# Attention probabilities transposed without TensorE, and a fixed instruction order from the fourth chunk

## The chip, the cores and the metric

The kernel runs on one core of one Trainium2 chip. The metric is the device time of one execution in microseconds. The kernel before took 1209.49 us (median of 3 runs, 1207.8 to 1210.51); it is called "before" below.

## What is computed

Two stages follow each other. The first is attention of 8 batches with 8 heads, head size 64: 512 local positions attend to 32 global keys and to a band of 32 positions on either side; 32 global positions attend to all 544 keys. The second is a gated feed-forward network on all 8 × 544 = 4352 tokens, with model width 512 and inner width 1536.

```python
s_g = scale * np.matmul(q_g, k_all.transpose(0, 1, 3, 2));  out_g = np.matmul(sm(s_g), v_all)
s_ll = np.where(np.abs(pos[:, None] - pos[None, :]) <= 32, scale * q_l @ k_l^T, -1e9)
out_l = np.matmul(sm(concat([q_l @ k_g^T * scale, s_ll])), concat([v_g, v_l]))
x = concat([out_g, out_l]).transpose(0, 2, 1, 3).reshape(B * S, 512)
y = (1 / (1 + np.exp(-(x @ w_gate))) * (x @ w_val)) @ w_out
```

All of it is float32. The kernel writes a float32 operand as a rounded high part plus the rest ("hi" and "lo", type fp32r) and adds three of the four products.

## The kernel before

**Chunks.** The tokens are worked on in chunks of 512 (one batch of local tokens; batch 0 is cut into two chunks of 256, numbers 0 and 1; batches 1 to 7 are chunks 2 to 8), and the 256 global tokens come last. While the feed-forward network of one chunk runs on TensorE, the attention of the next chunk is threaded between its matmuls. The network of a chunk is a loop over 12 slices f of the inner width: 12 matmuls into bank_g and 12 into bank_v (line 385), ScalarE's Tanh, Exp and Abs and two VectorE operations make th, ScalarE and GpSimd split it into hh, and one slice later 12 matmuls (line 414) add it into the four banks bank_o. From chunk 2 on a matmul has 512 columns.

**A local unit.** A head has two local units of two 128-row query blocks each and one global unit. Heads of chunks 0 and 1 and heads 0 to 3 of chunk 2 are "native" (plain float32); the other 52 heads, 104 local units, are split into hi and lo. A local unit goes through four stages of `local_unit`: the scores (line 229, and in a head's second unit two small products of line 223), VectorE's mask and row minimum (241), ScalarE's Exp (244); the reciprocal of the row sum and the scaling by it (252, 253, 208); four TensorE transposes of 128 × 128 (264, 265) into the PSUM tile bank_y, and the split of the result into pt by ScalarE (274) and VectorE (275); four matmuls with the values (294, 295), ScalarE's copy of the lower half (297), VectorE's and GpSimd's additions (298, 299), which give x32. Two heads later `x_split` writes xt, the input of the next chunk's network. The global unit (line 330 and following) interleaves its scores with the previous head's global products (308).

**What sets the order.** Attention steps are events with a due time. The unit of time is four 512-column matmuls of the network: `ffn_stream` yields after every four, and every event that has come due by then is issued. A head's base time is 12 units after the one before it; its local units are 4 units apart, and the four stages of a unit stand 0, 3, 6 and 9 units behind its start (`STAGES`). All the instructions of a stage are issued at once. A scheduler then sets each engine's final order by its own estimates.

**Queues and buffers.** Every DMA is issued by SyncE (SP), in order. PSUM tiles bank_g, bank_v, bank_x and bank_y share four banks (tag "att"); pt has two buffers, s_buf three, ob (the output rows) four.

Of the kernel before, what the change touches and what calls it, by code (L numbers as in the profile page):

```python
# [37 lines left out]
BASE, PER = 3, 4  # L38
STAGES = (0, 3, 6, 9)
LOAD_QK, LOAD_V, SPLIT_QK, SPLIT_V = 16, 9, 10, 4  # L40
# [15 lines left out]
def kernel(ctx, tc, qk, v, w_gate, w_val, w_out, out_l, out_g):  # L56
# [28 lines left out]
    ident_r, masks_r = (const.tile([P, w], F32R, name=nm) for w, nm in ((P, "ident_r"), (256, "masks_r")))  # L85
    nc.scalar.copy(ident_r, ident)
    nc.scalar.copy(masks_r, masks[:, 0:256])
# [101 lines left out]

    def split_v(T):  # L190
        if T["native"]:
            return
        t = T["v_raw"]
        vhl = spl.tile([P, 8, 2 * D], F32R, name="vhl")
        nc.scalar.copy(vhl[:, :, 0:D], t)  # L195
        nc.gpsimd.tensor_tensor(vhl[:, :, D:2 * D], t, vhl[:, :, 0:D].bitcast(F32), op=ALU.subtract)  # L196
        T["v"] = vhl

    def warm(bank, n):

        for _ in range(n):
            nc.tensor.matmul(bank[:, 0:256], ident_r, masks_r, start=True, stop=True)
# [8 lines left out]
    def local_unit(T, blocks, x32s, h, col0):  # L211
        ks, k0s, q0 = T["qk"], T["k0"], T["q0"]
        nat = T["native"]
        last = len(ks) - 1
        s_ps = ps.tile([P, 2, 256], F32, name="bank_x", tag="att", bufs=4)
        if T["first"]:
            warm(s_ps.rearrange("p a c -> p (a c)"), 16 if h == 0 else 2)
        with_gg = T["with_g"] and blocks[-1] == 3
        if with_gg:

# [4 lines left out]
        for i, j in enumerate(blocks):  # L225
            qj = ks[0][:, qcol(j) - q0:qcol(j) - q0 + P]
            for t, (kt, k0) in enumerate(zip(ks, k0s)):
                js = slice(k0 + KOFF[j], k0 + KOFF[j] + KWIN[j])
                nc.tensor.matmul(s_ps[:, i, 0:KWIN[j]], qj, kt[:, js], start=t == 0, stop=t == last)  # L229
        if T["first"] and cnt["s"] % 2:  # L230
            s_sb = ffn.tile([P, 2, WIN], F32, name="s_first", tag="ob", bufs=4)
# [4 lines left out]
        nm = small.tile([P, 2], F32, name="nm")  # L236
        sm = small.tile([P, 2], F32, name="sm")
        r = small.tile([P, 2], F32, name="r")
        for i, j in enumerate(blocks):
            w, m = KWIN[j], 0 if j else WIN  # L240
            anchor[0] = nc.vector.tensor_tensor_reduce(  # L241
                out=s_sb[:, i, 0:w], in0=s_ps[:, i, 0:w], in1=masks[:, m:m + w], scale=-0.125, scalar=3.0e38,
                op0=ALU.add, op1=ALU.min, accum_out=nm[:, i:i + 1])
            nc.scalar.activation(s_sb[:, i, 0:w], s_sb[:, i, 0:w], AF.Exp, bias=nm[:, i:i + 1], scale=-1.0,  # L244
                                 accum_out=sm[:, i:i + 1])
        if with_gg:
            mg = T["mg"] = small.tile([SG, 4], F32, name="mg")
            nc.vector.tensor_tensor_reduce(
                out=pg[:, SL:GW], in0=gg, in1=zero.broadcast_to([SG, SG]), scale=-0.125, scalar=3.0e38,
                op0=ALU.add, op1=ALU.min, accum_out=mg[:, 0:1])  # L250
# [15 lines left out]
        if nat:  # L266
            if T["first"] and h % 2:
                pt = ffn.tile([P, 4, P], F32, name="pt_first", tag="th", bufs=2)
            else:
                pt = att.tile([P, 4, P], F32, name="pt_nat", tag="pt", bufs=2)  # L270
            nc.scalar.copy(pt, pt_ps)
        else:
            pt = att.tile([P, 2, 4, P], F32R, name="pt", bufs=2)
            nc.scalar.copy(pt[:, 0], pt_ps)  # L274
            nc.vector.tensor_tensor(pt[:, 1], pt_ps, pt[:, 0].bitcast(F32), op=ALU.subtract)  # L275
# [5 lines left out]
        dst = x32s[h // 2][prow:prow + 64, col0:col0 + 2 * P].rearrange("p (i c) -> p i c", c=P)
        if nat:
            if T["first"]:
                o_ps = ps.tile([64, 2, P], F32, name="bank_x", tag=f"bank_o{2 + h % 2}")
            else:
                o_ps = ps.tile([64, 2, P], F32, name="bank_x", tag="att", bufs=4)
            for i, j in enumerate(blocks):
                nc.tensor.matmul(o_ps[:, i], vt[:, VM[j], :], pt[:, 2 * i], start=True, stop=False)  # L288
                nc.tensor.matmul(o_ps[:, i], vt[0:sides[i], VS[j], :], pt[0:sides[i], 2 * i + 1], start=False, stop=True)
            nc.scalar.copy(dst, o_ps)  # L290
# [299 lines left out]
```

## Time and profile before

| what | value |
|---|---|
| median of the runs | 1209.49 us |
| the profiled execution, its own time and its span | 1206.77 us, 1204.7 us |
| busy: PE, DVE, ACT, POOL | 97%, 60%, 65%, 49% of the span |
| mean granted TensorE clock | 0.987 |
| DMA | 152.80 MB, mean 127 GB/s |
| end of the network of chunk 2, of chunk 3 | 402.3 us, 532.9 us |

The span runs from the first instruction to the last; the profiled execution's own time is 2.1 us more than it. PE's busy share includes the time in which a matmul's result is still on its way, so the distance between starts tells what a matmul takes from PE, and the durations do not. "PEld" is the loading of weights, which overlaps matmuls.

### The profile page before, as it was taken

To read this page: it belongs to the slowest core of one execution; us is meant where nothing else is said; L and a number is where in the kernel's file an instruction comes from. 1 tells how busy PE (TensorE), PEld (TensorE's weight loads), DVE (VectorE), ACT (ScalarE), POOL (GpSimd) and SP (SyncE) were. 2 spreads that over 40 slices of the span, in tenths; PEclk is the share of its full clock that TensorE was granted. 3 is DMA by queue.
4 is the path that set the end of the run, shared out by engine and by line. 5 is a ranking of instruction groups with operands and counts; after the bars stand their busy time and mean duration, and the time that the engine had idled before them with its cause. 6 is when DMAs were issued, how large, how long until landed. Compare 5 with 4: busy or idle time off the path is not lost.

```text
span 1204.7 us, 19673 instructions
## 1 busy us (share of the span) xinstructions
PE 1172.4 (97%) x6606; PEld 971.4 (81%) x6606; DVE 727.5 (60%) x2275; ACT 780.2 (65%) x1836; POOL 585.4 (49%) x631
## 2 busy tenths in 40 slices
PE   8887999999999999999999999999999999999998
PEld 7565778888888888888888888888888888888897
DVE  5866874756776567756765677757775677511121
ACT  6766786767677677767766767767776776532232
POOL 2442553645656366545656465636654565311111
PEclk9978899999999999999999999999999999999999
DMA  7674763433334433333334433443434332131143
GB/s 259 237 270 166 253 210 105 118 120 112 98 103 130 125 105 123 97 127 105 115 97 123 125 95 110 127 128 100 128 97 127 106 114 75 53 105 55 68 145 119
DMA packets 50277, 152.80 MB, mean 127 GB/s; under 512 B 6144, under 2 KB 7168, under 8 KB 50176
## 3 DMA queue, kind: packets, MB, share of 16 engines
q1 hardware_dynamic: 50176, 151.54, 40.2%
q8 instruction: 52, 0.85, 0.3%
q14 instruction: 49, 0.40, 0.1%
HBM read 136.31 MB, written 15.20 MB: 126 GB/s over the span
## 4 chain that ended last, share of the span: by engine, by line
PE 75%; ACT 8%; DVE 7%; issue 6%; POOL 2%; DMA 1%; SPq 0%; POOLq 0%; ACTq 0%; DVEq 0%
PE bank_g L385 20%; PE bank_o L414 19%; PE bank_v L385 18%; PE bank_x L229 5%; PE bank_x L330 3%; PE bank_x L294 2%; PE bank_y L264 2%; PE bank_y L265 2%; PE bank_x L295 2%; ACT s_buf L244 1%; PE bank_x L308 1%; DVE s_buf L208 1%; ACT pg_buf L343 1%; POOL hh L401 1%; PE bank_x L288 1%
## 5 line engine op out<-in xcount | busy, mean ns | idle before, releaser
L385 PE MATMUL bank_g<-xt,wg 128*128 128x512 f32 (+1 forms) x1440 | 337.2, 369 | 1.0 <-ACT xt L367 0.9
L385 PE MATMUL bank_v<-xt,wv 128*128 128x512 f32 (+1 forms) x1440 | 329.1, 364 | 0.0
L414 PE MATMUL bank_o<-wo,hh 128*128 128x512 f32 x1224 | 325.0, 399 | 0.3 <-ACT hh L400 0.2
L385 PEld LDWEIGHTS bank_g<-xt,wg 128*128 128x128 f32 x1440 | 239.6, 191 | 41.6 <-issue 3.0
L385 PEld LDWEIGHTS bank_v<-xt,wv 128*128 128x128 f32 x1440 | 236.3, 188 | 38.0 <-issue 1.1
L414 PEld LDWEIGHTS bank_o<-wo,hh 128*128 128x128 f32 x1224 | 219.2, 189 | 41.7 <-issue 1.1
L401 POOL TENSOR_TENSOR hh<-th,hh 128x512 fp32r<-128x512 f32 (+1 forms) x120 | 136.7, 1139 | 237.8 <-ACT hh L400 226.8
L397 DVE SCALAR_TENSOR_TENSOR bank_v<-ex,bank_v 128x512 f32<-128x512 f32 (+1 forms) x120 | 73.1, 610 | 152.1 <-PE bank_v L385 148.7
L184 POOL TENSOR_TENSOR kl<-qk_raw,qk_hi 128x736 fp32r<-128x736 f32 x52 | 92.2, 1773 | 132.9 <-ACT qk_hi L183 131.8
L244 ACT ACTIVATE s_buf<-s_buf,nm 128x192 f32<-128x192 f32 (+1 forms) x248 | 114.1, 461 | 50.2 <-DVE nm L241 47.8
L400 ACT CAST hh<-th 128x512 fp32r<-128x512 f32 (+1 forms) x120 | 66.6, 555 | 115.4 <-DVE th L398 114.7
L393 ACT ACTIVATE th<-bank_g 128x512 f32<-128x512 f32 (+1 forms) x120 | 63.4, 528 | 83.5 <-PE bank_g L385 82.6
L241 DVE CUSTOM_DVE_ANT_0 s_buf<-bank_x,masks 128x192 f32<-128x192 f32 (+1 forms) x248 | 82.3, 367 | 41.9 <-PE bank_x L229 40.4
L299 POOL TENSOR_TENSOR x<-t 64x256 f32<-64x256 f32 x104 | 77.0, 740 | 62.0 <-DVE t L298 59.4
L196 POOL TENSOR_TENSOR vhl<-v_raw,vhl 128x512 fp32r<-128x512 f32 x52 | 67.0, 1288 | 47.8 <-ACT vhl L195 45.8
L208 DVE TENSOR_SCALAR s_buf<-s_buf,r 128x224 f32<-128x224 f32 (+1 forms) x230 | 86.1, 396 | 3.8
L183 ACT CAST qk_hi<-qk_raw 128x1280 fp32r<-128x1280 f32 x52 | 65.8, 1266 | 29.1 <-PE bank_x L308 17.8
L275 DVE TENSOR_TENSOR pt<-bank_y,pt 128x512 fp32r<-128x512 f32 x104 | 71.5, 687 | 20.6 <-ACT pt L274 20.0
L298 DVE TENSOR_TENSOR t<-bank_x,t 64x512 f32<-64x512 f32 x104 | 70.7, 680 | 21.0 <-ACT t L297 17.3
L186 POOL TENSOR_TENSOR qk_hi<-qk_raw,qk_hi 64x256 fp32r<-64x256 f32 x104 | 78.8, 772 | 4.7
L252 DVE TENSOR_SCALAR r<-sm 128x2 f32<-128x2 f32 x128 | 33.5, 262 | 78.2 <-ACT s_buf L244 78.2
L398 DVE SCALAR_TENSOR_TENSOR th<-th,bank_v 128x512 f32<-128x512 f32 (+1 forms) x120 | 72.4, 603 | 6.1 <-DVE bank_v L397 0.5
(117 smaller groups left out, 2003.1 us busy)
## 6 DMA issues: line engine op xcount, KB each, us to landing
wo<-wo_dram SPq DMA_DIRECT2D x116, 512.0 KB, 3.3
qk_raw<-in_qk_dram SPq DMA_DIRECT2D x104, 320.0 KB, 4.6
v_raw<-in_v_dram SPq DMA_DIRECT2D x52, 256.0 KB, 2.6
out_dram<-ob SPq DMA_DIRECT2D x34, 256.0 KB, 3.0
xt<-in_w_gate_dram SPq DMA_DIRECT2D x12, 512.0 KB, 4.5
xt<-in_w_val_dram SPq DMA_DIRECT2D x12, 512.0 KB, 4.1
xt<-in_w_out_dram SPq DMA_DIRECT2D x12, 512.0 KB, 4.2
v_nat<-in_v_dram SPq DMA_DIRECT2D x8, 512.0 KB, 3.9
```

The costliest lines, as they stand in the source:

```text
L184: nc.gpsimd.tensor_tensor(kl, t[:, K0:Q1], hi[:, K0:Q1].bitcast(F32), op=ALU.subtract)
L186: nc.gpsimd.tensor_tensor(hi[64:128, r], t[64:128, r], hi[64:128, r].bitcast(F32), op=ALU.subtract)
L208: nc.vector.tensor_scalar(out, in_, by, None, op0=ALU.mult)
L241: anchor[0] = nc.vector.tensor_tensor_reduce(out=s_sb[:, i, 0:w], in0=s_ps[:, i, 0:w], in1=masks[:, m:m + w], scale=-0.125, scalar=3.0e38, ...
L244: nc.scalar.activation(s_sb[:, i, 0:w], s_sb[:, i, 0:w], AF.Exp, bias=nm[:, i:i + 1], scale=-1.0, accum_out=sm[:, i:i + 1])
L275: nc.vector.tensor_tensor(pt[:, 1], pt_ps, pt[:, 0].bitcast(F32), op=ALU.subtract)
L299: nc.gpsimd.tensor_tensor(dst, t0[:, :, 0], t0[:, :, 1], op=ALU.add)
L385: nc.tensor.matmul(acc, w[a][:, t, fs], xt[:, c, t, x0:x0 + ntok], start=n == 0, stop=n == 11)
L397: nc.vector.scalar_tensor_tensor(acc, ex, 1.0, acc, op0=ALU.min, op1=ALU.mult)
L398: nc.vector.scalar_tensor_tensor(th, th, 1.0, acc, op0=ALU.add, op1=ALU.mult)
L401: nc.gpsimd.tensor_tensor(hh[:, 1, 0:ntok], th, hh[:, 0, 0:ntok].bitcast(F32), op=ALU.subtract)
L414: nc.tensor.matmul(o_ps[t], ph[:, a, t * P:(t + 1) * P], pwo[:, c], start=f2 == 0 and i == 0, stop=f2 == NF - 1 and i == 2)
```

## The change

**The transposes.** In the split units `local_split` takes the place of `local_unit`. The four TensorE transposes and bank_y are gone. VectorE transposes both blocks' probabilities inside each 32 × 32 square (one instruction, 128 × 448, into the new tile tb, two buffers); four DMAs write tb into a DRAM buffer pd (three buffers) in rows of 64 numbers, 256 bytes each; two DMAs read pd back as 128 rows of 1 KB each, already in the order that the products need, into the half pt[:, 1]. ScalarE makes the hi half from it, and the subtraction that leaves the lo half is done in place, by GpSimd in a head's first unit and by VectorE in its second. The products read pt in runs of 32 numbers.

**The order.** From due time 108 on (the network of chunk 2, the attention of chunk 3) every engine's order is the order in which the program issues: the scheduler no longer moves anything. Each unit is cut into smaller steps with delays of their own (`LOCAL`, `GLOBAL`, `LAST`, `SPLIT`, in the same units of time), and a head starts 5 units earlier against the network (`BASE` 3 becomes -2).

**Smaller edits.** ob has three buffers in place of four; the warming matmuls at the start have 128 columns in place of 256 and are twice as many; the tile masks_r is gone.

```diff
-BASE, PER = 3, 4
+BASE, PER = -2, 4
+MANUAL = 108
+LOCAL = dict(reduce=0.5, exp=0.4, norm=1.7, write=1.3, read=4, hi=4, lo=0.6, pv=2, copy=0.5, add=0.6, x=0.7)
-        for i in range(2):
-            nc.tensor.transpose(pt_ps[:, 2 * i], s_sb[:, i, 0:P], ident)
-            nc.tensor.transpose(pt_ps[:, 2 * i + 1], s_sb[:, i, WIN - P:WIN], ident)
...
-            pt = att.tile([P, 2, 4, P], F32R, name="pt", bufs=2)
-            nc.scalar.copy(pt[:, 0], pt_ps)
-            nc.vector.tensor_tensor(pt[:, 1], pt_ps, pt[:, 0].bitcast(F32), op=ALU.subtract)
+        tb = att.tile([P, 7, 2, 32], F32, name="tb", bufs=2)
+        nc.vector.transpose(tb.rearrange("p b k i -> p k b i"), s_sb.rearrange("p k (b i) -> p k b i", i=32))
+        yield w["write"]
+        pd = dram.tile([7, 32, 4, 64], F32, name="pd", bufs=3)
+        for a in range(4):
+            rows = slice(32 * a, 32 * a + 32)
+            nc.sync.dma_start(pd[:, :, a].rearrange("b j r -> j b r"), tb[rows].rearrange("p b k i -> p b (k i)"))
+        yield w["read"]
+        pt = att.tile([P, 2, 2, 4, 2, 32], F32R, name="pt", bufs=2)
+        for m in range(2):
+            src = pd[3 * m:3 * m + 4].rearrange("b j a r -> (b j) (a r)")
+            nc.sync.dma_start(pt[:, 1, m].rearrange("p a k i -> p (a k i)").bitcast(F32), src)
+        yield w["hi"]
+        flat = pt.rearrange("p c m a k i -> p c (m a k i)")
+        nc.scalar.copy(flat[:, 0], flat[:, 1].bitcast(F32))
+        yield w["lo"]
+        (nc.vector if blocks[0] else nc.gpsimd).tensor_tensor(
+            flat[:, 1], flat[:, 1].bitcast(F32), flat[:, 0].bitcast(F32), op=ALU.subtract)
+        yield w["pv"]
...
+            nc.tensor.matmul(out, vt[:, VM[j], :], pt[:, :, 0, :, i, :], start=True, stop=False)
+            nc.tensor.matmul(out, vt[0:side, VS[j], :], pt[0:side, :, 1, :, i, :], start=False, stop=True)
...
-                            ob = ffn.tile([P, DM], F32, name="ob", bufs=4)
+                            ob = ffn.tile([P, DM], F32, name="ob", bufs=3)
...
+    def step(gen):
+        d = next(gen, None)
+        if d is not None:
+            put(now[0] + d, 2, lambda: step(gen))
+    def start(gen, at_once=True):
+        if now[0] >= MANUAL or not at_once:
+            step(gen)
+        else:
+            for _ in gen:
+                pass
...
     for dt in ffn_stream(items):
-        now += dt
-        while queue and queue[0][0] <= now:
-            queue.pop(0)[2]()
+        catch_up(now[0] + dt)
+        if now[0] >= MANUAL and MANUAL not in cnt:
+            cnt[MANUAL] = region.enter_context(tc.manual_schedule())
+    region.close()
```

**How the order moves.** First TensorE, in the middle of a chunk, around one slice's matmuls into bank_v (wv) and bank_o. Before, a unit's four transposes (lines 264, 265, read from s_buf) stand between them:

```order
L385 MATMUL bank_v<-xt,wv_118 128x512 x3
L264 MATMUL bank_y<-ident,s_buf_107 128x128 [waits DVE_49]
L265 MATMUL bank_y<-ident,s_buf_107 128x128
L264 MATMUL bank_y<-ident,s_buf_107 128x128 [waits DVE_49]
L265 MATMUL bank_y<-ident,s_buf_107 128x128
L385 MATMUL bank_v<-xt,wv_119 128x512 x4
```

After, network matmuls, a unit's scores (231) and another unit's products (353, 354) are all that is there, and the products carry a wait on DMA queues beside those on engines:

```order
L231 MATMUL bank_x<-qk_hi 128x192 [waits DVE_49]
L231 MATMUL bank_x<-kl,qk_hi 128x192
L231 MATMUL bank_x<-qk_hi 128x224
L231 MATMUL bank_x<-kl,qk_hi 128x224
L487 MATMUL bank_g<-xt,wg_114 128x512 x4
L487 MATMUL bank_v<-xt,wv_116 128x512 [waits DVE_49]
L487 MATMUL bank_v<-xt,wv_116 128x512 x3
L487 MATMUL bank_v<-xt,wv_117 128x512 x4
L353 MATMUL bank_x<-pt,vhl 128x256 [waits DMAHW6_49,DVE_49,Pool_49]
L354 MATMUL bank_x<-pt,vhl 128x256 [waits DMAHW7_49]
L353 MATMUL bank_x<-pt,vhl 128x256
L354 MATMUL bank_x<-pt,vhl 128x256
```

From the scores of a unit to its own products PE now has 60 network matmuls of 512 columns, two other units' scores (one of them with the two small products), two other units' products and one global unit with its products; before, the due times put 9 units (36 network matmuls) between them.

Second, SyncE's queue, for about one head in the middle of a chunk. Before:

```order
L405 DMA wo<-wo_dram_129 128x1024 [waits DMAHW5_49,PE_49]
L174 DMA v_raw<-in_v_dram 128x512 [waits DMAHW2_49,Pool_49]
L405 DMA wo<-wo_dram_130 128x1024 [waits DMAHW1_49,PE_49]
L159 DMA qk_raw<-in_qk_dram 64x1280 [waits DMAHW4_49,DMAHW3_49,Pool_49]
L159 DMA qk_raw<-in_qk_dram 64x1280
```

After, the writes of probabilities (335) and the reads (340) stand among them:

```order
L335 DMA pd<-tb 32x7x64 [waits DVE_49]
L335 DMA pd<-tb 32x7x64
L335 DMA pd<-tb 32x7x64 [waits DMAHW4_49]
L335 DMA pd<-tb 32x7x64 [waits DMAHW5_49]
L340 DMA pt<-pd 128x256 [waits DMAHW4_49,DMAHW3_49,DMAHW5_49,DMAHW2_49,DMAHW6_49,PE_49,Pool_49]
L340 DMA pt<-pd 128x256 [waits DMAHW7_49]
L335 DMA pd<-tb 32x7x64 [waits DMAHW0_49,DVE_49]
L335 DMA pd<-tb 32x7x64 [waits DMAHW1_49]
L335 DMA pd<-tb 32x7x64 x2
L165 DMA qk_raw<-in_qk_dram 64x1280 [waits Activation_49,Pool_49]
L506 DMA wo<-wo_dram_124 128x1024 [waits DMAHW6_49,PE_49]
L340 DMA pt<-pd 128x256 [waits DMAHW2_49,DMAHW1_49,DMAHW3_49,DMAHW0_49,DMAHW7_49,PE_49,Activation_49]
```

The first read of a unit waits in the queue until the unit's four writes have landed; the next unit's writes and the next head's loads of q and k stand behind it.

More of the change, by code (lines that the diff above doesn't have):

```diff
@@ L1 @@
-from contextlib import nullcontext
+from contextlib import ExitStack, nullcontext
+from heapq import heappush, heappop
 import concourse.bass as bass
@@ L83 @@
     nc.scalar.copy(masks[:, WIN + P + 32:WIN + 192], masks[:, P + 64:WIN])
-    ident_r, masks_r = (const.tile([P, w], F32R, name=nm) for w, nm in ((P, "ident_r"), (256, "masks_r")))
+    ident_r = const.tile([P, P], F32R, name="ident_r")
     nc.scalar.copy(ident_r, ident)
-    nc.scalar.copy(masks_r, masks[:, 0:256])
     s_bufs = [const.tile([P, 2, WIN], F32, name=f"s_buf{i}") for i in range(3)]
@@ L209, in scaled, with local_scores @@
         cnt["norm"] += 1
-    def local_unit(T, blocks, x32s, h, col0):
+    def local_scores(T, blocks, s_ps):
         ks, k0s, q0 = T["qk"], T["k0"], T["q0"]
-        nat = T["native"]
         last = len(ks) - 1
[L215 to L219, printed above, removed]
+        if T["with_g"] and blocks[-1] == 3:
             gg = s_ps[0:SG, 0, WIN:]
@@ L235, in local_unit @@
         cnt["s"] += 1
-        nm = small.tile([P, 2], F32, name="nm")
-        sm = small.tile([P, 2], F32, name="sm")
-        r = small.tile([P, 2], F32, name="r")
+        nm, sm, r = small_tiles()
         for i, j in enumerate(blocks):
[L240 to L250, printed above, removed]
+            local_reduce(i, j, s_sb, s_ps, nm)
+            local_exp(i, j, s_sb, nm, sm)
+        if T["with_g"] and blocks[-1] == 3:
+            own_reduce(T, s_ps)
         yield
@@ L280, in local_unit @@
         prow = 64 * (h % 2)
[L281 to L290, printed above, removed]
-            return
+        return x32s[h // 2][prow:prow + 64, col0:col0 + 2 * P].rearrange("p (i c) -> p i c", c=P)
@@ L425, in ffn_stream, with put, att_events @@
             prev = (C, f, hh, wo) if n_it < len(items) else None
-    def att_events(ci, start, per, tail=0):
+    queue, now, seq = [], [-1.0e9], [0]
+    def put(t, order, fn):
+        seq[0] += 1
+        heappush(queue, (t, order, seq[0], fn))
+    def step(gen):
[5 more added lines that the diff above has]
+            step(gen)
+        else:
+            for _ in gen:
+                pass
+    def att_events(ci, first, per):
         b, blocks, with_g = chunks[ci]
@@ L457, in att_events @@
             T = heads[h]
-            base = start + per * npu * h
+            base = first + per * npu * h
             sc = per / 4
```

241 lines of the change are left out of this document (173 added, 68 removed).

## The prediction

> **What bounds the kernel now.** I read the page's busy times first, then stretches of time in the middle, then TensorE's waits there, then the chain of waits for what a matmul really takes. The busy times (first two fences) name PE:
>
> ```profile
> span 1204.7 us, 19673 instructions
> PE 1172.4 (97%) x6606; PEld 971.4 (81%) x6606; DVE 727.5 (60%) x2275; ACT 780.2 (65%) x1836; POOL 585.4 (49%) x631
> ```
>
> The stretches (columns: from and to, length, then busy us of PE, PEld, DVE, ACT and POOL with counts, granted clock, DMA share, GB/s) show 130 us in the middle, with attention:
>
> ```profile
> 502.00:632.00 130.00, 129.49 (x711) 107.77 (x710) 86.94 (x282) 90.94 (x206) 73.88 (x81) 1.00 0.38 114
> ```
>
> VectorE's timeline gives the length of a chunk, from its writes of ob (line 422) at the ends of two chunks:
>
> ```profile
> 402.29 1.28 DVE L422 TENSOR_SCALAR ob<-bank_o 128x512 f32<-128x512 f32 x2
> ...
> 532.92 1.28 DVE L422 TENSOR_SCALAR ob<-bank_o 128x512 f32<-128x512 f32 x2
> ```
>
> That is 130.63 us per chunk, with six such chunks (the networks of 2 to 7). In the stretch 502 to 632, PE's groups show a single wait worth a number, 0.5 us:
>
> ```profile
> L330 PE MATMUL bank_x<-qk_hi 128*32 128x256 f32 x16 | 4.5, 284 | 0.5 <-ACT ex L394 0.5
> ```
>
> So PE is dense, and what it saves, the chunk saves. What a matmul takes is in the chain of waits (start, us, what), where each piece runs to the next start:
>
> ```profile
> 602.91 0.44 PE bank_x L229 x4
> 603.35 0.94 PE bank_v L385 x4
> 604.29 0.12 PE bank_x L294
> ...
> 607.52 0.05 PE bank_x L223 x2
> 607.57 0.52 PE bank_x L229 x4
> ...
> 609.97 0.11 PE bank_y L264
> 610.08 0.11 PE bank_y L265
> 610.19 0.11 PE bank_y L264
> 610.30 0.11 PE bank_y L265
> ...
> 625.48 0.92 ACT s_buf L244 x4
> ...
> 627.87 0.03 PE bank_x L308
> 627.90 0.12 PE bank_x L330
> ```
>
> Four network matmuls take 0.94 us, four transposes 0.44, a unit's scores 0.44 (first unit of a head) or 0.57, its four products 0.48, a global unit 4 × 0.12 + 5 × 0.03 = 0.63. A chunk needs 108 × 0.94 + 8 × (0.44 + 0.57) + 16 × (0.48 + 0.44) + 8 × 0.63 = 129.4 us of 130.63: 1.3 us per chunk is waiting, all told.
>
> **The change part by part.** *Transposes removed.* 104 units × 0.44 us = 45.8 us, 42 of it in the six chunks (96 units) and 3.5 in the heads 4 to 7 of chunk 2, where PE is also nearly full.
>
> The Trainium skill, TensorE: Matmul & The Clock Gate, section Part 4: PE-mode transpose, gives some 275 ns for a transpose inside a kernel; by it the saving would be 416 × 275 ns = 114 us, an estimate. The trace has that duration too (273 ns in the row of line 265 below), but the pieces of the chain start 0.11 us apart, and the starts decide.
>
> *Work that moves to other engines* (rows behind the first; groups by shape; after the bar busy us and mean ns, then idle time before):
>
> ```profile
> L265 PE MATMUL bank_y<-ident,s_buf 128*128 128x128 f32 x248 | 61.4, 273 | 0.0
> L275 DVE TENSOR_TENSOR pt<-bank_y,pt 128x512 fp32r<-128x512 f32 x104 | 71.5, 687 | 20.6 <-ACT pt L274 20.0
> L357 DVE STREAM_TRANSPOSE ptg_buf<-pg_buf 32x128 f32<-32x128 f32 x208 | 62.8, 302 | 3.4
> L354 DVE STREAM_TRANSPOSE ptg_buf<-pg_buf 32x32 f32<-32x32 f32 x52 | 10.5, 201 | 4.1 <-ACT pg_buf L343 2.3
> L401 POOL TENSOR_TENSOR hh<-th,hh 128x512 fp32r<-128x512 f32 x84 | 108.5, 1292 | 171.4 <-ACT hh L400 164.9 <-DMA qk_raw<-in_qk_dram 5.1
> L400 ACT CAST hh<-th 128x512 fp32r<-128x512 f32 x84 | 52.1, 620 | 94.3 <-DVE th L398 93.7
> ```
>
> VectorE's block transpose grows from 201 to 302 ns with 96 more columns, 1.05 ns each, so 448 columns take 0.64 us; 16 per chunk less 8 subtractions of 0.69 is +4.7 us, 91.6 of a chunk of 123.6. GpSimd gets 8 subtractions of 1.29 us: 84 of 123.6. ScalarE's copy stays as long (0.62). All three stay below 75% of a chunk, so none becomes the bound by its sum; PE hides them. If that cover went, they would cost PE what they are late, which is the next point.
>
> *The way round through DRAM.* The products are the waiting instruction: behind them in PE's queue stands the network. From the order, PE has 60 × 0.235 = 14.1 us of network, and 0.57 + 0.44 + 2 × 0.48 + 0.63 = 2.6 us of attention, between a unit's scores and its products: 16.7 us (before it was 36 network matmuls, 8.5 us, and some attention). What must fit in is the sum of these rows (the page's groups, then a group by shape, DMA issues and SP's timeline) with the rows above:
>
> ```profile
> L244 ACT ACTIVATE s_buf<-s_buf,nm 128x192 f32<-128x192 f32 (+1 forms) x248 | 114.1, 461 | 50.2 <-DVE nm L241 47.8
> L241 DVE CUSTOM_DVE_ANT_0 s_buf<-bank_x,masks 128x192 f32<-128x192 f32 (+1 forms) x248 | 82.3, 367 | 41.9 <-PE bank_x L229 40.4
> L208 DVE TENSOR_SCALAR s_buf<-s_buf,r 128x224 f32<-128x224 f32 (+1 forms) x230 | 86.1, 396 | 3.8
> L252 DVE TENSOR_SCALAR r<-sm 128x2 f32<-128x2 f32 x128 | 33.5, 262 | 78.2 <-ACT s_buf L244 78.2
> L253 DVE RECIPROCAL r<-r 128x2 f32<-128x2 f32 x128 | 20.8, 163 | 3.2
> ```
>
> ```profile
> wo<-wo_dram SPq DMA_DIRECT2D x116, 512.0 KB, 3.3
> qk_raw<-in_qk_dram SPq DMA_DIRECT2D x104, 320.0 KB, 4.6
> v_raw<-in_v_dram SPq DMA_DIRECT2D x52, 256.0 KB, 2.6
> out_dram<-ob SPq DMA_DIRECT2D x34, 256.0 KB, 3.0
> ```
>
> ```profile
> 602.56 0.34 SPq L174 DMA_DIRECT2D v_raw<-in_v_dram  x1
> 604.44 1.11 SPq L159 DMA_DIRECT2D qk_raw<-in_qk_dram  x2
> ```
>
> Engines: 2 × 0.37 (241) + 0.92 (the four pieces of line 244 in the chain) + 0.26 + 0.16 + 2 × 0.40 + 0.64 + 0.62 + 1.29 = 5.4 us. DMAs: four writes issued at 0.34 us each, the last landing after 3.0 us as ob's stores do, two reads issued, landing after 2.6 as v's loads do: 1.4 + 3.0 + 0.7 + 2.6 = 7.7 us. Together 13.1 of 16.7. The 11.3 us left for the DMAs shrink by queueing on three engines that are about 70% full; I allow 1.3 us for that (one subtraction of GpSimd ahead of ours) and call 10.0 us free. The low bound for the DMAs is 7.7; the high one, with every landing as late as that of q and k, 1.4 + 4.6 + 0.7 + 4.6 = 11.3. I take the value nearest in size, a 57 KB write and a 128 KB read being smaller than ob's and v's 256 KB: 7.7, cost nothing. SP's own queue: six more issues per unit, 12 per head on top of some 4.5, 16.5 × 0.34 to 0.55 = 5.6 to 9 us of a head's 13.7 (12 units of the due time): no bound, but the first read holds the queue until the writes have landed, so the next unit's writes and a q and k load are late by as much as the writes are.
>
> The Trainium skill, DMA: Bandwidth & Descriptors, section Rules for kernel authors, counts transfers under 64 KB as mostly overhead; with the fixed 2.0 us plus bytes over 436 GB/s of that page the way round would be 1.4 + 2.1 + 0.7 + 2.3 = 6.5 us, an estimate, a little better than mine. Its section Specifications speaks against the writes: below 512 bytes a packet is read, changed and written back. No run here shows that yet.
>
> *Load on the DMA engines.* A unit adds 896 packets of 256 bytes, 256 of 1 KB, and 96 endings of DMAs (16 each; the page's small packets are 16 × 384 DMAs):
>
> ```profile
> DMA packets 50277, 152.80 MB, mean 127 GB/s; under 512 B 6144, under 2 KB 7168, under 8 KB 50176
> ...
> q1 hardware_dynamic: 50176, 151.54, 40.2%
> ```
>
> That is 1248 a unit, 19968 a chunk. The bounds of a packet: 40.2% of 16 engines' 1204.7 us over 50176 packets is 154 ns (of 3 KB); by bytes, 19.6 GB/s per engine, the 7.86 MB of a chunk come to 20 ns each. A chunk uses 0.38 × 16 × 130 = 790 us now and has 16 × 123.6 = 1978; the engines are full at (1978 − 790) / 19968 = 59 ns. v's 256 KB land in 2.6 us, wo's 512 KB in 3.3, so time grows with bytes and not with packets (both have 128); I take 40 ns, twice the byte price, 80% full, and keep 154 as the far end, where a chunk would last (790 + 3075) / 16 = 242 us and the kernel near 1870.
>
> *The fixed order.* It can win back at most 1.3 us in six chunks, 8 us, and lose that again; I take nothing. *ob with three buffers:* a chunk's fourth store waits some 3 us for the first to land, on ScalarE, behind which stand the next Tanh and Exp; PE asks for that bank again 24 matmuls (5.6 us) later, so nothing, or 8 ends × 3 us without that cover. *The products' runs of 32 numbers:* line 330's reading in four pieces costs PE the same 0.12 us per 256 columns, so nothing. *Warming matmuls and masks_r:* the same columns in all, nothing. *The first 270 us* are laid out anew by the scheduler; PE's largest wait there (us in total, times, longest) is of native code:
>
> ```profile
> PE bank_y L348 <- ACT pg_buf L343: 13.0, 8, 2.9
> ```
>
> I allow plus or minus 8 us, some two thirds of it, and take nothing.
>
> *Sum:* the profiled execution's 1206.8 − 45.8 = 1161.0; the median of the runs is 2.7 above that execution (1209.5 against 1206.8), so 1164 us.
>
> **The rivals.** *The way round is late, slower than before.* Place: PE at line 353, its DMA wait. Each unit lasts 123.6 / 16 = 7.7 us, so 16.7 us hold 2.2 units, and an excess of e us over 10.0 is shared by them: e / 2.2 per unit. It eats the 0.44 saved at e = 1.0, a way round of 11.0 us. At 11.3 (all landings as q and k's): 1.3 / 2.2 × 96 = 57 us, 1164 + 57 = 1221. For it: seven times as many small packets, reads behind loads of q and k in one queue, engines 80% full. Against: the 13.1 us sum. *The same, but milder:* 10.5 us costs 0.5 / 2.2 × 96 = 22 us: 1186. *A better order:* no waits left in the chunks and 8 us gained at the start: 1148. *The change doesn't do what it says, nothing won:* the three engines, in a fixed order with the same lateness at each step, hold PE at the old 130.6 us per chunk, 1209; against it, none is over 75% full.
>
> **How the numbers follow.** Forecast (1150 to 1180) 0.60, the milder lateness (1180 to 1207) 0.16, slower than before 0.16, nothing won 0.05, the better order 0.03. What a measurement can't tell from no change is about 0.2%, 2.4 us. Faster: 0.60 + 0.16 + 0.03 = 0.79; same 0.05; slower 0.16. Range: from the better order, 1148, to 1214, which takes in the milder lateness, no change and the near end of the slower case, and leaves some 15% out; the forecast's own is 1150 to 1180.
>
> **What would show it.** Right: chunk ends 123 to 124 us apart, no bank_y in split units, products (353) without a DMA wait of weight, the DMA share near 0.65 to 0.8, reads of pd landing in under 3.5 us. Wrong: idle PE before line 353 released by DMA or by the subtraction of line 345, a packet over 59 ns (DMA share at 0.95), or PE waiting for PSUM behind a ScalarE that sits before line 343.

## The result, and the profile after

The change made the kernel slower: 1375.22 us (median of 3, 1374.2 to 1380.64) against 1209.49, a ratio of 1.1384 with an interval of 1.1334 to 1.1435. Predicted were 1164 us and a range of 1148 to 1214.

The page of the kernel after, its busy times, and the stretch between two ends of chunks (columns as in the prediction's stretches), with the two writes of ob that mark them:

```profile
span 1372.4 us, 20474 instructions
PE 1200.1 (87%) x6236; PEld 968.2 (71%) x6236; DVE 798.1 (58%) x2327; ACT 780.8 (57%) x1835; POOL 670.5 (49%) x683
...
617.91:768.62 150.71, 128.38 (x649) 102.31 (x648) 98.20 (x291) 91.41 (x206) 88.09 (x88) 0.99 0.52 151
...
617.91 1.25 DVE L523 TENSOR_SCALAR ob<-bank_o 128x512 f32<-128x512 f32 x2
768.62 1.25 DVE L523 TENSOR_SCALAR ob<-bank_o 128x512 f32<-128x512 f32 x2
```

A chunk takes 150.7 us instead of 130.6, and PE is idle for 22 of them; before, it was idle for half a microsecond. No other engine is full: VectorE is busy for 98 of 150.7 us, ScalarE for 91, GpSimd for 88. What has grown is the waiting.

The span grew by 167.7 us. By the writes of ob, chunk 1 ends at 316.0 us instead of 270.8 (45 us), the six chunks behind it take 902.6 us instead of 783.2 (119), and the rest 3 more. Two things have to be explained, then, not one.

The kernel's waits of PE, largest first (us in total, times, longest):

```profile
PE bank_x L353 <- POOL pt L345: 69.7, 36, 8.0
PE bank_x L353 <- DVE pt L345: 33.6, 28, 4.5
PE bank_x L353 <- issue: 16.6, 12, 1.4
```

That is the place which the prediction named for the slower rival: the products of line 353. But what they wait for is the subtraction of line 345 on GpSimd or VectorE; the profile puts none of it down to a DMA. For the 16.6 us of "issue" it names nobody, but in the one of these waits that I followed, the product starts at 803.91 us, 0.11 after the end of VectorE's subtraction.

Most of what the new operations themselves cost was as predicted. The page's groups, DMA issues and queue:

```profile
L330 DVE STREAM_TRANSPOSE tb<-s_buf 128x448 f32<-128x448 f32 x104 | 67.1, 645 | 3.5
L328 DVE TENSOR_SCALAR s_buf<-s_buf,r 128x224 f32<-128x224 f32 x104 | 58.6, 564 | 1.8
L345 DVE TENSOR_TENSOR pt<-pt 128x512 fp32r<-128x512 f32 x52 | 53.3, 1026 | 31.9 <-ACT pt L343 31.9
...
pt<-pd SPq DMA_DIRECT2D x208, 128.0 KB, 3.2
pd<-tb SPq DMA_DIRECT2D x416, 56.0 KB, 1.7
...
q1 hardware_dynamic: 179968, 202.70, 49.4%
```

The block transpose takes 0.645 us (0.64 predicted), the subtraction on VectorE 1.03 (0.69 predicted; see the last section). A write lands 1.7 us after its issue and a read 3.2; with 1.8 us for issuing four writes and 0.8 for two reads, the way round DRAM is 7.5 us (7.7 predicted). From the first write's issue to the last read's landing, the 16 units of the chunk took 7.9 us in the mean, 5.6 to 14.3, what the reads wait in SyncE's queue included.

One unit, followed through the engines' timelines of the kernel after (start, us, what; idle time before it in brackets), shows where the time went instead:

```profile
793.30 0.27 PE L231 MATMUL bank_x<-kl,qk_hi 128*128 128x224 f32 x1
...
794.34 0.14 DVE L417 TENSOR_SCALAR mg<-sg 32x1 f32<-32x1 f32 x1 [0.91 <-ACT pg_buf L413]
795.54 0.20 DVE L449 STREAM_TRANSPOSE ptg_buf<-pg_buf 32x32 f32<-32x32 f32 x1 [0.88 <-ACT pg_buf L447]
795.76 1.25 DVE L452 STREAM_TRANSPOSE ptg_buf<-pg_buf 32x128 f32<-32x128 f32 x4
797.04 0.36 DVE L235 CUSTOM_DVE_ANT_0 s_buf<-bank_x,masks 128x192 f32<-128x192 f32 x1
799.67 0.65 DVE L330 STREAM_TRANSPOSE tb<-s_buf 128x448 f32<-128x448 f32 x1
...
800.35 1.79 SPq L335 DMA_DIRECT2D pd<-tb  x4
803.58 0.81 SPq L340 DMA_DIRECT2D pt<-pd  x2
...
808.86 0.62 ACT L462 CAST xt<-x 128x512 fp32r<-128x512 f32 x1 [1.75 <-POOL x L361]
809.39 0.75 ACT L413 ACTIVATE pg_buf<-pg_buf,mg 32x544 f32<-32x544 f32 x1
810.68 0.75 ACT L447 ACTIVATE pg_buf<-pg_buf,mg 32x544 f32<-32x544 f32 x1 [0.45 <-DVE mg L418]
811.33 0.60 ACT L343 CAST pt<-pt 128x512 fp32r<-128x512 f32 x1
...
812.01 1.29 POOL L345 TENSOR_TENSOR pt<-pt 128x512 fp32r<-128x512 f32 x1
813.36 0.39 PE L353 MATMUL bank_x<-pt,vhl 128*128 128x256 f32 x1 [0.15 <-POOL pt L345]
```

The scores are there at 793.57. VectorE could reduce them at once, and begins at 797.04: ahead of them in its queue stands the global unit's softmax, which goes from VectorE to ScalarE and back twice (lines 407, 413, 417, 447, 449), and VectorE stands idle at its head, 0.91 and 0.88 us, while the scores are ready. From there to the transposed tile it takes 3.3 us. The two reads are issued by 804.4 and land, by the median, 3.2 us after issue, the second at about 807.2; ScalarE rounds them at 811.33, some 4.1 us late, because ahead of it in that queue stand the rounding of x, which itself waited 1.75 us for GpSimd, and the global softmax of the next head. The whole way is 19.8 us, of which the unit's own steps and DMAs are some 12.2 and waiting in queues 7.6 (3.5 before the reduction, 4.1 before the rounding). Over the 16 units of the chunk the mean, read in the same way, is 20.8 us. The two waits have the same weight there: 3.4 us from the scores to the reduction (0.04 to 6.9) and 3.4 us from the landing of the last read to the rounding (0.2 to 6.7).

### The profile page after: what moved, and what is told of

It is laid out like the page before. It is cut to its first block, busy times and chain, and to the rows that moved or that the text cites. A ratio compares the mean times of both kernels' runs of the same rounds, so it can differ in the third digit from the quotient of the medians.

```text
span 1372.4 us, 20474 instructions
## 1 busy us (share of the span) xinstructions
PE 1200.1 (87%) x6236; PEld 968.2 (71%) x6236; DVE 798.1 (58%) x2327; ACT 780.8 (57%) x1835; POOL 670.5 (49%) x683
## 4 chain that ended last, share of the span: by engine, by line
PE 35%; DVE 20%; ACT 15%; issue 11%; POOL 9%; DMA 6%; SPq 2%; DVEq 0%; POOLq 0%; ACTq 0%
PE bank_v L487 9%; PE bank_g L487 8%; PE bank_o L515 6%; ACT s_buf L241 3%; DVE s_buf L328 3%; PE bank_x L231 3%; DVE pt L345 3%; PE bank_x L399 2%; DMA qk_raw<-in_qk_dram 2%; POOL hh L470 2%; DVE bank_v L499 2%; DVE t L359 2%; DVE th L500 2%; DVE ptg_buf L452 2%; POOL x L361 2%
## 5 line engine op out<-in xcount | busy, mean ns | idle before, releaser
L487 PE MATMUL bank_g<-xt,wg 128*128 128x512 f32 (+1 forms) x1440 | 332.2, 372 | 7.2 <-ACT xt L462 6.3
L487 PEld LDWEIGHTS bank_g<-xt,wg 128*128 128x128 f32 x1440 | 247.4, 196 | 53.7 <-ACT xt L462 9.2
L515 PEld LDWEIGHTS bank_o<-wo,hh 128*128 128x128 f32 x1224 | 231.3, 197 | 50.4 <-POOL hh L470 1.8
L353 PE MATMUL bank_x<-pt,vhl 128*128 128x256 f32 x208 | 66.2, 338 | 120.4 <-POOL pt L345 69.7
L353 PEld LDWEIGHTS bank_x<-pt,vhl 128*128 128x128 f32 x208 | 41.4, 199 | 155.8 <-POOL pt L345 87.3
L361 POOL TENSOR_TENSOR x<-t 64x256 f32<-64x256 f32 x104 | 85.3, 820 | 95.5 <-DVE t L359 76.1
L328 DVE TENSOR_SCALAR s_buf<-s_buf,r 128x192 f32<-128x192 f32 x208 | 103.1, 536 | 3.6
L195 POOL TENSOR_TENSOR qk_hi<-qk_raw,qk_hi 64x256 fp32r<-64x256 f32 x104 | 88.0, 866 | 4.2
L345 POOL TENSOR_TENSOR pt<-pt 128x512 fp32r<-128x512 f32 x52 | 66.3, 1275 | 46.5 <-ACT pt L343 45.8
L413 ACT ACTIVATE pg_buf<-pg_buf,mg 32x544 f32<-32x544 f32 x64 | 47.7, 745 | 66.4 <-DVE mg L407 66.3
```

What stands on the lines that cost most here:

```text
L328: nc.vector.tensor_scalar(s_sb[:, i, 0:KWIN[j]], s_sb[:, i, 0:KWIN[j]], r[:, i:i + 1], None, op0=ALU.mult)
L345: (nc.vector if blocks[0] else nc.gpsimd).tensor_tensor(flat[:, 1], flat[:, 1].bitcast(F32), flat[:, 0].bitcast(F32), op=ALU.subtract)
L353: nc.tensor.matmul(out, vt[:, VM[j], :], pt[:, :, 0, :, i, :], start=True, stop=False)
L361: nc.gpsimd.tensor_tensor(x_part(x32s, h, col0), t0[:, :, 0], t0[:, :, 1], op=ALU.add)
L487: nc.tensor.matmul(acc, w[a][:, t, fs], xt[:, c, t, x0:x0 + ntok], start=n == 0, stop=n == 11)
L515: nc.tensor.matmul(o_ps[t], ph[:, a, t * P:(t + 1) * P], pwo[:, c], start=f2 == 0 and i == 0, stop=f2 == NF - 1 and i == 2)
```

## The experiments

Four parts of the change are separable: the way round DRAM, the fixed order with its due times, the warming matmuls, and the three buffers of ob.

**DRAM under the scheduler's own order.** The fixed order is left off throughout.

```diff
-MANUAL = 108
+MANUAL = 10**9
```

> The changed kernel with the scheduler's order to the end (the fixed region never begins); transposes still by VectorE and DRAM. If the fixed order is what costs (every engine holds its queue for whatever is late), TensorE's wait at line 353 falls from 120 us to under 30, a chunk from 150 us to 126 to 132, and the whole to about 1250 us (the 45 us lost before 316 us stay). If the way round through DRAM is too long for any order, a chunk stays at 145 or more and the whole at 1340 to 1400.

Measured: 1488.36 us, ratio 1.2271 [1.2156, 1.2387], chunks of 170.7 us, above both expectations. The way round DRAM is worse in the scheduler's order than in the fixed one: the products wait there 112.8 us for VectorE's subtraction and 68.1 us for GpSimd's. DRAM itself is hardly slower (8.5 us a unit in one chunk, 7.9 in the kernel after); what is late is the rounding, 8.5 us behind the landing instead of 3.4. So the fixed order doesn't spoil a good order for this version; for it, it is the better of the two. This run also shows something of the clock, told in the last section.

**The fixed order with TensorE's transposes.** Transposes as before the change, in the fixed order, with due times made shorter by the DRAM steps.

```diff
-BASE, PER = -2, 4
+BASE, PER = 3, 4
-LOCAL = dict(reduce=0.5, exp=0.4, norm=1.7, write=1.3, read=4, hi=4, lo=0.6, pv=2, ...)
+LOCAL = dict(reduce=0.5, exp=0.4, norm=1.7, turn=1.8, hi=0.8, lo=0.6, pv=2, ...)
-        (block transpose, four writes, two reads)
+        (four tensor.transpose into bank_y, subtraction from bank_y)
```

> The fixed order from the fourth chunk with TensorE's transposes as before (no block transposes, no DRAM), steps delayed as in the change where they are the same, BASE 3 as before. If the fixed order is what costs, a chunk is 140 us or more (before 130.6) and the whole 1300 or more. If the way round through DRAM costs, a chunk is 129 to 133 and the whole about 1250, of which some 45 us are lost before the fixed region.

Measured: 1340.32 us, ratio 1.1051 [1.096, 1.1141], chunks of 148.5 us. With no DRAM at all nearly the whole lengthening of a chunk is there. The waits are many and short:

```profile
PE bank_x L344 <- DVE pt L338: 32.8, 25, 1.5
PE bank_y L332 <- DVE y L373: 17.5, 24, 0.8
PE bank_y L332 <- DVE s_buf L328: 13.3, 21, 1.8
```

Since the due times were my own and short, this left open whether they or a fixed order as such did it; two runs below bear on that, the fixed order alone and other due times.

**ob with three buffers**, alone in the kernel before.

```diff
-            s_sb = ffn.tile([P, 2, WIN], F32, name="s_first", tag="ob", bufs=4)
+            s_sb = ffn.tile([P, 2, WIN], F32, name="s_first", tag="ob", bufs=3)
-                            ob = ffn.tile([P, DM], F32, name="ob", bufs=4)
+                            ob = ffn.tile([P, DM], F32, name="ob", bufs=3)
```

> The kernel before with three ob buffers in place of four, nothing else. The change lost 45 us by the end of chunk 1 (316 against 271 us), where the fixed order has not begun; the starting chunk uses ob's buffers for its scores. If the missing buffer does it, the first network matmul moves from 29 to about 46 us, chunk 1 ends near 310 and the whole takes about 1250 us; if the scheduler's new layout does it, the time stays within 5 us of 1209.

Measured: 1215.02 us, ratio 1.0002 [0.9955, 1.0049]. Nothing, as predicted.

**More slack for the products.** In the kernel after, products 4 units (3.8 us) later, attention 4 units earlier, v's split later.

```diff
-BASE, PER = -2, 4
+BASE, PER = -6, 4
-LOAD_QK, LOAD_V, SPLIT_QK, SPLIT_V = 16, 9, 10, 4
+LOAD_QK, LOAD_V, SPLIT_QK, SPLIT_V = 16, 9, 10, 1
-        w = LOCAL
+        w = dict(LOCAL, pv=LOCAL["pv"] + (4 if T["late"] else 0))
```

> The changed kernel with the products of a unit due 4 units (some 4.5 us of matmuls) later in the fixed region, heads starting 4 units earlier against the network, and the values split 3 units later so that its buffer is free. If lateness at line 353 is the whole cost, its wait falls from 120 us to under 20, a chunk to 124 to 130 us and the whole to 1200 to 1250 us. If the fixed order's queues are what is slow, the wait moves to other places and the whole stays above 1320.

Measured: 1387.45 us, ratio 1.1439 [1.1347, 1.1532], chunks of 151 us. The wait at the products shrank, and as much appeared elsewhere:

```profile
PE bank_x L399 <- DVE mg L246: 30.6, 18, 2.5
PE bank_x L399 <- DVE th L500: 18.7, 6, 4.7
PE bank_v L487 <- ACT ex L496: 18.2, 12, 1.6
PE bank_x L353 <- POOL pt L345: 18.0, 4, 8.0
```

So more time for the products alone doesn't help; I read it so, that room at one place is lost when the queues ahead of it stay as they are.

**The fixed order alone.** The kernel before with nothing else changed; from the same point on, every engine keeps the order in which the program is written.

```diff
+    region = ExitStack()
     for dt in ffn_stream(items):
         ...
+        if now >= 108 and not fixed:
+            fixed = True
+            region.enter_context(tc.manual_schedule())
+    region.close()
```

> The kernel before, with nothing changed but the order: from the same point as in the changed kernel every engine keeps the program's own order. Theory 1 (the order written down is what costs: each engine waits in its queue for the late head, whatever does the transposes): chunk ends move from 130.6 to about 150 us apart as in the changed kernel, and the kernel takes 1320 to 1350 us. Theory 2 (the way round through DRAM and the subtraction behind it cost; an order alone is harmless): chunks within 3 us of 130.6, kernel 1205 to 1230 us.

Measured: 1371.28 us, ratio 1.1313 [1.1238, 1.1389]. The order alone, with TensorE's transposes, the old warming and the old buffers, costs 160 us, more than I had expected. The stretch of one chunk and PE's first waits:

```profile
595.96:752.59 156.63, 138.79 (x713) 110.28 (x712) 90.86 (x283) 91.91 (x208) 74.67 (x81) 0.97 0.33 95
...
PE bank_y L264 <- DVE s_buf L208: 34.5, 30, 3.3
PE bank_g L385 <- ACT xt L367: 19.0, 7, 3.4
PE bank_y L264 <- DVE y L315: 14.2, 12, 1.6
```

The same instructions that the scheduler packs into 130.6 us take 156.6 when their written order is kept. Before the change the scheduler was worth 26 us per chunk. This written order isn't that of the changed kernel, though: here all the instructions of a stage are issued at once, there in smaller steps.

**No DRAM in the kernel after.** Writes and reads left out; rounding and subtraction read VectorE's tile directly, so the attention isn't the reference's.

```diff
-        (pd, its four writes and two reads)
+        src = tb_bufs[cnt["tb"] % 2] (taken before the transpose)
-        nc.scalar.copy(flat[:, 0], flat[:, 1].bitcast(F32))
+        nc.scalar.copy(flat[:, 0], src)
```

> The changed kernel without the four writes and the two reads of a unit: ScalarE's rounding and the subtraction read VectorE's transposed tile directly, so the wait for DRAM and the load on the queue are gone, and the attention it computes is not the reference's (the blocks are not gathered). Every engine's own instructions, due times and the fixed order stay. If the 7.6 us of DRAM are the late step: PE's wait at the products goes from 120 us to under 15 and chunks last 126 to 132 us, kernel 1190 to 1260. If the queues of the engines are what is late (VectorE's and GpSimd's own instructions, in a fixed order): chunks stay at 143 to 150 us, kernel 1320 to 1375.

Measured: 1360.25 us, ratio 1.1222 [1.1156, 1.1289], chunks of 150.4 us; the products still wait 63.0 us for GpSimd's subtraction and 51.0 for VectorE's. This agrees with the queues and not with DRAM, but it is weaker than it looks: with two tiles in turn the rounding takes the tile that was written last, that of a later unit, which is a wait of its own that the changed kernel doesn't have. I don't rest the verdict on it.

**Warming matmuls of 128 columns**, alone in the kernel before.

```diff
-            nc.tensor.matmul(bank[:, 0:256], ident_r, masks_r, start=True, stop=True)
+            nc.tensor.matmul(bank[:, 0:P], ident_r, ident_r, start=True, stop=True)
-            warm(..., 16 if h == 0 else 2)    and 2
+            warm(..., 32 if h == 0 else 4)    and 4
```

> The kernel before with the warming matmuls of the changed one alone: twice as many, of 128 columns instead of 256. If a matmul of 128 columns takes as long as one of 256 (0.22 us each against 0.236 in the two profiles' first group), the first scores come 2.4 us later, the 46 more warming matmuls cost 8 to 15 us, chunk 1 ends 8 to 20 us later and the kernel takes 1218 to 1230 us. If columns alone count, as I predicted: within 3 us of the kernel before.

Measured: 1234.58 us, ratio 1.019 [1.0142, 1.0238]. PE's first rows in the kernel before, its first network matmul, and its stretch from 50 to 150 us:

```profile
3.37 3.78 PE L202 MATMUL bank_x<-masks_r,ident_r 128*128 128x256 f32 x16 [3.37 <-ACT masks_r L87]
29.17 0.40 PE L385 MATMUL bank_g<-xt,wg 128*128 128x256 f32 x2
...
50.00:150.00 100.00, 84.48 (x492) 65.34 (x492) 72.62 (x189) 71.12 (x187) 40.99 (x34) 0.85 0.68 231
```

The same with the other warming:

```profile
2.37 7.09 PE L202 MATMUL bank_x<-ident_r 128*128 128x128 f32 x32 [2.37 <-ACT ident_r L86]
46.27 0.99 PE L385 MATMUL bank_g<-xt,wg 128*128 128x256 f32 x3
...
50.00:150.00 100.00, 90.45 (x451) 67.60 (x450) 61.06 (x168) 62.69 (x168) 32.33 (x27) 0.68 0.61 205
```

A matmul of 128 columns takes 0.22 us there, one of 256 columns 0.24: twice the number costs nearly twice the time. The first network matmul comes 17 us later, the granted clock from 50 to 150 us is 0.68 instead of 0.85, and chunk 1 ends at 294.7 instead of 270.8, 24 us later, somewhat more than the 8 to 20 expected: half of the 45 lost at the start. Why the clock stays lower there these runs don't show.

**The low half on ScalarE.** In the kernel after the subtraction is replaced by a copy on ScalarE, so the low part is wrong, and neither VectorE nor GpSimd has that step.

```diff
-        (nc.vector if blocks[0] else nc.gpsimd).tensor_tensor(
-            flat[:, 1], flat[:, 1].bitcast(F32), flat[:, 0].bitcast(F32), op=ALU.subtract)
+        nc.scalar.copy(flat[:, 1], flat[:, 1].bitcast(F32))
```

> The changed kernel with the subtraction of the low half left out: ScalarE writes a copy there, 0.62 us a unit more for ScalarE, so the low part of the probabilities is wrong. VectorE and GpSimd lose 1.07 and 1.29 us per unit of theirs, and no longer read the same memory for it. If the subtraction is what is late (GpSimd's queue 69.7 us and VectorE's 33.6 us of PE's wait at the products) and what delays VectorE's next reductions: chunks of 130 to 138 us, kernel 1240 to 1300. If DRAM or the order is what is late, the wait goes over to ScalarE: chunks of 146 to 152 us, kernel 1350 to 1380.

Measured: 1337.61 us, ratio 1.1036 [1.0964, 1.1107], chunks of 146 us, between the two expectations and nearer to the second. The wait goes over to ScalarE, 76.6 us at the same products. A shorter step on another engine (0.62 us instead of 1.03 and 1.28) wins back 5 of the 20 us per chunk, so neither the subtraction's length nor its engine is the main part.

**Other due times, nothing else.** The kernel after with other numbers in the tables that place each step (the network's split scaled by 0.3 for its narrow items).

```diff
-BASE, PER = -2, 4
+BASE, PER = -8, 4
-LOCAL = dict(reduce=0.5, exp=0.4, norm=1.7, write=1.3, read=4, hi=4, lo=0.6, pv=2, copy=0.5, add=0.6, x=0.7)
+LOCAL = dict(reduce=0.05, exp=0.4, norm=1.7, write=1.3, read=4, hi=3.8, lo=1.8, pv=2, copy=0.5, add=1.0, x=0.35)
-GLOBAL = dict(reduce=1.3, exp=0.6, norm=0.9, scale=0.3, turn=0.7, hi=1.4, lo=0.4)
+GLOBAL = dict(reduce=0.8, exp=0.6, norm=1.5, scale=0.05, turn=1.62, hi=1.4, lo=0.7)
-SPLIT = dict(qk=1.1, v=0.6, x=0.6, h=1.2, hl=0.6)
+SPLIT = dict(qk=0.8, v=0.6, x=0.42, h=1.6, hl=3.9)
 (and LAST, LOAD_*, SPLIT_*, HOLE by small amounts)
```

> The changed kernel with nothing else changed than the numbers that set where each step stands in the fixed order (due times): reductions right behind their scores, the subtraction of the low half 1.2 units later, the network's split later (1.6 and 3.9 units instead of 1.2 and 0.6), attention 6 units earlier against the network. Theory 1 (the loss is where the steps stand in the engines' queues, not the way round through DRAM nor a fixed order as such): chunks of 128 to 134 us, stalls of PE at the products under 0.5 us a unit, kernel 1235 to 1275 us. Theory 2 (the instructions' own load on VectorE and GpSimd, or DRAM, sets the pace): chunks stay at 145 us or more, kernel above 1335.

Measured: 1277.63 us, ratio 1.0521 [1.0448, 1.0595], against 1.1384 with the old numbers; 3 us above the range of theory 1, and far from that of theory 2. DRAM, transposes, instructions and buffers are the same; only their places differ. A chunk, and PE's waits:

```profile
725.00:857.90 132.90, 125.63 (x650) 101.81 (x649) 100.64 (x291) 91.03 (x208) 88.47 (x89) 1.00 0.62 170
...
PE bank_x L353 <- POOL pt L345: 35.9, 31, 6.0
PE bank_y L430 <- ACT pg_buf L426: 11.2, 7, 3.0
```

This chunk is 18 us shorter than the one above (the six chunks of this run last 129 to 139 us, 133.9 in the mean, against 150.4 before these numbers), and 98 us in all are won back by the places alone. Over the 16 units of this chunk the scores wait 1.4 us for their reduction instead of 3.4 and the landed tile 0.9 for its rounding instead of 3.4, while the way round DRAM takes 8.3 us, not less than the 7.9 of the kernel after. Which of the numbers did it this run doesn't tell, since they were changed together (the products also have 64 network matmuls behind their scores now instead of 60, 0.9 us more room); what PE waits for most is still GpSimd's subtraction, half as long.

**The same due times with the old start.** Warming of 256 columns (its operand kept in hh's place) and TensorE's transposes for heads 4 to 7 of chunk 2, which the scheduler orders.

```diff
+            if T["pe"]:   # chunk 2
+                (transposes on TensorE, as before)
-            nc.tensor.matmul(bank[:, 0:P], ident_r, ident_r, start=True, stop=True)
+            nc.tensor.matmul(bank[:, 0:256], ident_r, masks_r, start=True, stop=True)
```

> The same due times, with the warming matmuls of 256 columns as before the change, and TensorE's transposes kept in the one chunk that the scheduler still orders (heads 4 to 7 of chunk 2). If the start's loss is the warming (24 us by the run of it alone) and the way round DRAM under the scheduler (some 15 us by the chunk ends of the runs so far), this ends at 1195 to 1235 us. If the start's loss is something else, it stays within 10 us of the run with the due times alone.

Measured: 1237.66 us, ratio 1.0202 [1.0147, 1.0257], 3 us above the first expectation. Chunk 1 ends at 279.4 instead of 317.1 us: 38 us come back, 24 of them the warming by its own run, and 14 by difference those four heads, whose DRAM steps the scheduler had placed. The run with TensorE's transposes in the fixed order agrees: it has the 128-column warming and the three buffers too, and its chunk 1 ends at 299.2 us, 17 before that of the kernel after. One chunk:

```profile
552.90:685.30 132.40, 125.67 (x651) 101.88 (x650) 100.41 (x291) 91.28 (x208) 88.43 (x88) 1.00 0.64 172
```

This is the fastest version with the new transposes that I found, and it is still 2% slower than the kernel before: its six chunks last 129 to 139 us, 133.6 in the mean, against 130.5. No version that beats the kernel before came out of these runs.

## Why the prediction was wrong

**The step that failed** is the one on the fixed order: "It can win back at most 1.3 us in six chunks, 8 us, and lose that again; I take nothing." With it failed the allowance for the same queues, "I allow 1.3 us for that". I had bounded what the order can win by the waiting left in the kernel before, and took the same number as the bound of what it can lose. There is no such bound: in the kernel before an order chosen by the scheduler was what kept PE dense, and to give it up costs 26 us per chunk by itself (the fixed order alone, 1.1313). In the changed kernel a unit waits 6.8 us in the mean in the queues of VectorE and ScalarE (3.4 before the reduction, 3.4 before the rounding) where 1.3 were allowed; with other due times it waits 2.3, and the same instructions and DMAs take 98 us less. VectorE and ScalarE were idle for some 40 us of each chunk before, and I read that as room. It doesn't follow that the scheduler should have been kept: with the way round DRAM its own order is worse still (chunks of 170.7 us). The loss lies in where the steps stand, and no run has a place for them that beats the kernel before.

**The sum of the engines.** "All three stay below 75% of a chunk, so none becomes the bound by its sum; PE hides them." The sums were near (VectorE 98 us where I had 91.6, GpSimd 88 where I had 84, ScalarE 91 as before; 65%, 58% and 61% of the longer chunk) and the conclusion wrong. An engine that takes its instructions in a fixed order isn't free when it is idle: VectorE stood idle at line 417 with a unit's scores ready behind it.

**The way round DRAM.** 7.7 us predicted for it, 7.5 measured by the medians and 7.9 over the chunk; 5.4 us for the engines' steps, close to the rows. In the unit above queueing cost 7.6 us. The rival's formula then fits: 20.8 us where 16.7 were free is 4.1 too much, over 2.2 units 1.9 us per unit; measured are (150.7 − 123.6) / 16 = 1.7. That agreement is bookkeeping and no test, since the 20.8 us are PE's own 16.7 and whatever PE waits in between; that these waits are mostly those of the products is read from the list of waits. I had the right place, the right rule and the right rival, and gave it the wrong mechanism (landings as late as those of q and k) and so a small chance. Its break-even, 1.0 us of excess, was far below what I didn't know about three queues.

**The transposes removed.** 0.44 us a unit, 7 a chunk. In the best version PE is busy for 125.7 us of the chunk shown, against 130.1 in the stretch from 402.29 to 532.92 us of the kernel before: 4.4 less. The first product after each wait lasts 0.36 to 0.39 us instead of 0.28, so the 2.6 that are missing lie at least in part in the waits themselves.

**Load on the DMA engines.** I took 40 ns for an added packet. The share in a chunk rose from 0.38 of 130 us to 0.52 of 150.7: 464 us more on 16 engines for 19968 packets, 23 ns each, nearly the 20 ns by bytes. At 0.64 in the densest version the engines aren't full. The Trainium skill, DMA: Bandwidth & Descriptors, section Specifications, has packets below 512 bytes read, changed and written back; no cost of that shows here, a 56 KB write of such packets landed in 1.7 us.

**The warming.** "The same columns in all, nothing": 24 us. Columns were the wrong unit; matmuls of 128 and 256 columns take nearly the same time there (0.22 and 0.24 us).

**The first 270 us**, plus or minus 8: 45 us later, 24 from the warming, some 14 to 17 from the four heads of chunk 2, and the rest not told apart (chunk 1's end moved by 10 us, 270.8 to 281.3, between the profiles of the kernel before and of its fixed order alone, whose start is the same).

**ob with three buffers:** nothing, as predicted.

**What I said would show it wrong** did: idle PE ahead of line 353, released by the subtraction of line 345. The added packets took 23 ns each in the mean, not 59, and there was no wait for a DMA of weight.

## What to carry to other kernels

Taking work off the engine that is full helps only if every queue behind it can take the longer way in time; add up the waits in the queues, not the busy times. What an order written by hand can lose is not bounded by today's waits: measure it by itself, on the unchanged kernel, before anything is built on it. And a place that an engine stands idle at, with ready work behind it, is found in its timeline, not in its share.

## What the hardware showed that I had not expected

**Half a period of idle TensorE, some 1.7 us, halves the granted clock behind it.** In the run with the scheduler's order the idle time before a matmul and the clock behind it go together. Three matmuls of PE's timeline and the stretches behind them (last three columns: granted clock, DMA share, GB/s):

```profile
645.99 0.39 PE L353 MATMUL bank_x<-pt,vhl 128*128 128x256 f32 x1 [1.40 <-DVE pt L345]
708.07 0.39 PE L353 MATMUL bank_x<-pt,vhl 128*128 128x256 f32 x1 [1.81 <-POOL pt L345]
715.15 0.58 PE L353 MATMUL bank_x<-pt,vhl 128*128 128x256 f32 x1 [3.27 <-DVE pt L345]
716.17 1.91 PE L487 MATMUL bank_g<-xt,wg 128*128 128x512 f32 x4
...
646.00:648.00 2.00, 2.00 (x13) 1.79 (x13) 0.54 (x1) 0.58 (x1) 1.08 (x1) 1.00 0.00 0
708.00:712.00 4.00, 3.82 (x16) 2.70 (x16) 3.28 (x12) 2.53 (x7) 1.97 (x3) 0.67 0.19 48
714.00:716.00 2.00, 0.84 (x4) 0.85 (x5) 1.10 (x1) 0.00 (x0) 1.92 (x3) 0.50 0.61 151
716.00:718.00 2.00, 2.00 (x8) 1.61 (x8) 0.64 (x1) 0.58 (x1) 0.45 (x1) 0.50 0.69 155
720.00:722.00 2.00, 2.00 (x11) 1.58 (x10) 0.51 (x3) 1.37 (x4) 1.48 (x2) 1.00 1.01 251
```

Behind 1.40 us the clock stays at 1.00; behind 1.81 it falls to 0.50 within 2 us and, with another wait of 3.27 us on the way, stays there until 719.6: four network matmuls take 1.7 us, from 716.17 to 717.88, instead of 0.94. From 330 to 1050 us of this run none of the twelve waits of 1.34 to 1.40 us was followed by a lower clock within 8 us, and every one of 1.8 us or more was, for 3.41 or 6.83 us, or 10.24 where two such waits fell close together. In the same stretch of the kernel after, waits of 1.54 to 1.59 us left the clock alone, one of 1.76 halved it, one of 2.27 did not, and the five above 4 us did. The traces' clock records say why length alone doesn't decide. All changes of the clock lie on a grid of 3.41 us, and what counts is PE's busy time within one such period: from 300 to 1100 us of all twelve traces, each of the 89 periods at full clock that were followed by half clock had PE busy for at most 0.48 of it, and each of the 2610 that were not had at least 0.50. The wait of 1.76 us lay within one period; that of 2.27 us was split by the grid into 1.16 and 1.11. So a wait is paid for again: the chunks of this run had a mean clock near 0.88, those of the densest version 1.00. It is also why it matters how waits are spread, not only their sum: the many short waits of the fixed order with TensorE's transposes left PE busy for at least 0.55 of every period, and its clock at 1.00. The Trainium skill, TensorE: Matmul & The Clock Gate, section Part 1: The HAM clock gate, tells of half rate after an idle window of some 3.4 us. The half rate agrees, and the idle time that is enough was half of that here.

**VectorE's work from SBUF to SBUF is slower while GpSimd works.** The instructions of line 328 in the kernel after (shortest, median and longest, in ns):

```profile
L328 DVE TENSOR_SCALAR s_buf<-s_buf,r x208: 306/336/1764, 221.7 to 1191.9; 128x192 f32<-128x192 f32 x52, 128x224 f32<-128x224 f32 x52
```

The same normalisation takes 0.31 us or up to 1.76. Of the 208, the 92 during which GpSimd ran nothing took 0.31 to 0.34 us; the 116 beside an operation of GpSimd took 0.31 to 1.76, 0.70 in the mean. The low half's subtraction, which now reads SBUF instead of PSUM, took 1.03 us on VectorE, nearly always beside GpSimd, where line 275 took 0.69 before. I had priced it by the row with a PSUM source. The source alone doesn't make it longer: the few that had GpSimd idle (one in this kernel, six in the run with the scheduler's order) took 0.69 us too; and line 275, reading PSUM, took 0.69 with and without GpSimd beside it. The Trainium skill, SBUF — State Buffer, section Who interferes with whom, has the two engines share a pair of ports under an exclusive lock. The rows with and without a neighbour agree with that; no run here took the neighbour away on purpose, so that the ports are the cause is argued, not shown.
